# First chunks held by ScalarE, scores by first rows, masks ahead of a running sum, and an opening in needed order

## The chip, the cores and the metric

The kernel runs on one core of a Trainium2 chip. The core has five engines that run side by side and meet only at semaphores: TensorE (PE in the profile; its weight loads are PEld), VectorE (DVE), ScalarE (ACT), GpSimd (POOL) and SyncE (SP), which here only issues transfers. The metric is the time of one execution on the device, in microseconds (us): 380.94 before, the median of 3 runs (380.69 to 381.0).

## The reference

Four batches, eight heads, 768 tokens, 48 channels a head. A gated recurrence gives y, and a feed-forward block with a softmax gate (SoLU) and a layer norm follows:

```python
for t in range(S):
    state = alpha[:, :, t, :, None] * state + np.einsum('bhd,bhe->bhde', k[:, :, t], v[:, :, t])
    y[:, :, t] = np.einsum('bhd,bhde->bhe', q[:, :, t], state)
# x = y, transposed to (3072 tokens, 384)
h = x @ w_in
e = np.exp(h - h_max)
solu = h * e / sum(e)
ln = (solu - mean(solu)) / np.sqrt(var(solu) + 1e-06) * g_ln
out = ln @ w_out
```

The weights `w_in` (384x1024), `w_out` (1024x384) and `g_ln` come as 64-bit floats; everything in the kernel is 32-bit.

## The kernel before, in words

**Groups and chunks.** Time is cut into six groups g of 128 tokens for all four batches b at once (512 columns). The 128 tokens of one batch are a chunk, number n = 4g + b. A group goes through attention, then `up` (h = x times w_in, eight pieces f of 128 hidden units, each with an Exp on ACT, a product on DVE and a Square on ACT: `up_act`), then `down` (four chunks of 128 x 385, each in two halves of four matmuls) and `finish`.

**Attention of a group.** The decay alpha is scanned backwards (`scan_back`, which fills `hT`) and forwards (`scan_on`, in place in `aT`) on DVE. Keys are multiplied by the first scan, queries by the second. The 48 channels of a head are split into 32 "first" rows and 16 "last" rows; tiles have 12 blocks, 8 of first rows (one a head) and 4 with the last rows of two heads. First rows of the queries are `qv[:, 0:8]`; last rows are in `qe`, from which ACT (`apart`) makes two masked copies, for even and for odd heads, in `qv[:, 8:16]`. `scores(g, half)` makes the token by token products of four heads on PE, in four PSUM banks (a0 to a3, one a batch): per head first rows, then last rows added on. `masked(half)` multiplies each bank by a triangle on DVE into `sT`, which frees the bank. `read_state` and `read_values` (L326) then make y from the old state and from `sT`; ACT copies y to `x` (L356), the input of `up`. `next_state` makes the new state; `decay` (GpSimd, L261) multiplies the old one. For `read_state` and `decay`, queries and the ends of the decay are copied by SyncE's transfers into `q64` (lot<-qe by `move_lasts`, lot<-qv by `move_firsts`), a part of the buffer `lot`.

**Getting channels on partitions.** In groups 0 and 1, `turned` transposes k and q on PE (alpha too in group 0), with the last rows gathered by ACT first (`ends_of`); later groups use DVE's transposes (`alpha_T` does it for alpha, with a memset of GpSimd ahead).

**The feed-forward's sums.** `running(g, f)` adds up e and its square over the pieces: one sum on GpSimd, one on DVE (L418). `finish(n)` takes the 385th column of the chunk's result (a sum over hidden units), makes the variance in small DVE instructions (L516 to L521), in group 0 adds the mean's part (L525), takes a power on GpSimd (L529), scales on ACT (L531) and sends the output from SyncE (L532). For group 0, `w_out` isn't centred yet; `centre(f)` does that on GpSimd in group 1.

**Buffers that tie these together.** PSUM has eight banks: two for `h`, two for `o` (results of `down`, also used by other tiles), four `a0` to `a3`. `down(n)` can only begin when the result of chunk n - 2 has been read out of its bank. `o_mean` and `o_sb` have two buffers each, so `finish(n)` reuses those of `finish(n - 2)`.

**What sets the order.** It is written by hand; each engine runs its instructions in program order. Group 0 and the start of group 1 are straight code (L640 to L812). There, the weights come in pieces of 64-bit words into `room` and DVE converts them (`bits`), between all else. From group 1's `up` on, a loop over g and f calls `attend` by a table: `usual`, and `first` for g = 1, say what stands at the head of piece f, behind its `up`, in the middle (after `running`) and at the tail. In the loop's pass g, `up` works on group g and attention on group g + 1, so that the masks and scores named by `first` are those of group 2. `warm` issues matmuls whose results nobody reads.

Of the kernel before, what the change touches and what calls it, by code (L numbers as in the profile page):

```python
# [9 lines left out]
FP = mybir.dt.float32  # L10
# [6 lines left out]
P = 128  # L17
# [15 lines left out]
def fast_path(ctx, tc, q, k, v, alpha, moe_w_in, moe_w_out, moe_g_ln, out):  # L33
# [231 lines left out]
    def quarter(b):  # L265
        return slice(32 * b, 32 * b + 32)
# [4 lines left out]
    def scores(g, half, a=None):  # L271
        a = a or banks("a", [NP, P])
        for i in range(NP):
            h = half * NP + i
            for kb, qb in ((h, h), (H + h // 2, H + h)):
                for b in range(B):
                    nc.tensor.matmul(  # L277
                        a[b][:, i], lhsT=kT[quarter(b), kb], rhs=qv[quarter(b), qb, 0:P], start=kb == h, stop=kb != h,
                        tile_position=(32 * b, 0), skip_group_check=True,
                    )  # L280
        masks[half] = a
# [158 lines left out]
    def warm(n, ps=ps_o, tag="o"):  # L440
        t = ps.tile([P, 512], FP, tag=tag, name="warm")
        for i in range(n):
            nc.tensor.matmul(t[:, 0:P], lhsT=ones, rhs=ones, start=True, stop=True)
# [48 lines left out]
    def down(n, half, part=range(HF)):  # L492
# [4 lines left out]
        for f in (half * HF + i for i in part):  # L497
# [3 lines left out]
            )  # L501

    def finish(n):
        g, b = divmod(n, B)
        d = st[n]
        s, o = sums[:, n], d["o"][:, 0:DM]
        t0 = b * S + g * P
        if g == G - 1:
# [6 lines left out]
            return  # L515
        nc.vector.tensor_copy(out=s[:, 0:1], in_=d["o"][:, DM : DM + 1])  # L516
        t = small.tile([P, 1], FP, name="t")
# [4 lines left out]
        if g == 0:  # L522

            o = work.tile([P, DM], FP, name="o_mean")
            nc.vector.scalar_tensor_tensor(  # L525
                out=o, in0=mean_sb, scalar=s[:, 0:1], in1=d["o"][:, 0:DM], op0=ALU.mult, op1=ALU.add
            )
        r = small.tile([P, 1], FP, name="r")
        nc.gpsimd.tensor_tensor(out=r, in0=s[:, 3:4], in1=mhalf, op=ALU.pow)  # L529
# [136 lines left out]
    def three(name, where):  # L666
        return [pool.tile([P, NP, P], FP, tag=tag, name=f"{name}{i}") for i, (pool, tag) in enumerate(where)]
# [16 lines left out]
    scan_on(0, 0)  # L684
    t = three("tp_q", [(ps_o, "o"), (ps_o, "o"), (ps_a, "a0")])
    turned(qn, ends_of(qn, 3), t)
    for i in (2, 0, 1):
        if i == 1:
            scan_on(0, i)
        part = slice(NP * i, NP * i + NP)  # L690
        nc.vector.tensor_tensor(  # L691
            out=qe[:, :, 0:P] if i == 2 else qv[:, part, 0:P], in0=t[i], in1=aT[:, part, 1:SW], op=ALU.mult
        )
        if i == 2:
            apart()
    warm(2, ps_a, "a1")
    scores(0, 0)
# [79 lines left out]
    move_lasts()  # L777
    finish(0)
    in_range(7)
# [23 lines left out]
    for i in range(3):  # L803
# [5 lines left out]
    down(3, 1, (2, 3))  # L809
    finish(3)  # L810
    scan_on(2, 2)
# [76 lines left out]
    for g in range(1, G + 1):  # L888
# [6 lines left out]

        after = None
        if not rise:
# [520 lines left out]
```

## Time and profile before

| | |
|---|---|
| median of 3 runs | 380.94 us |
| the profiled execution | 380.75 us |
| its span | 378.9 us |
| PE busy | 362.4 us (96%) |
| DVE busy | 246.0 us (65%) |
| ACT busy | 144.7 us (38%) |
| GpSimd busy | 120.5 us (32%) |
| granted TensorE clock, mean | 0.998 |

The span runs from the first to the last instruction that the profiler shows. Times in timelines are from its start. In a timeline a line gives start, length, engine, line of the source, operation, what it writes and reads, shape, count, and in brackets the idle time of the engine before it with what ended it. A wait inside a run of merged instructions doesn't show in brackets. In a table of stretches, each engine has its busy us and its instructions, and the last three numbers are the granted clock, the busy share of the transfer engines and GB/s.

### The profile page before, as it was taken

Reading aid. Unit: us, or ns where it says so; the run is one execution under the profiler, and the core shown is the slowest. Engines: PE = TensorE matmul, PEld = TensorE weight load, DVE = VectorE, ACT = ScalarE, POOL = GpSimd, SP = SyncE. Lnnn points to the kernel's source line nnn. Section 1 sums busy time; section 2 is a strip of 40 time slices with the busy share of each in tenths; the row PEclk is TensorE's granted clock in tenths of the full one; section 3 lists DMA queues with packets and bytes.
Section 4 is the critical chain, followed back from the end, with each engine's and each line's share of the span. In section 5 each row is a group of like instructions: output and inputs, shape, how many; then the busy total and the mean of one; then the engine's idle time right before and its main releaser. Section 6 shows DMA issues by size and latency. Waiting matters only on the chain. (4 is left out here: it accounts for less than half of the span.)

```text
span 378.9 us, 10022 instructions
## 1 busy us (share of the span) xinstructions
PE 362.4 (96%) x4337; PEld 215.1 (57%) x4337; DVE 246.0 (65%) x377; ACT 144.7 (38%) x256; POOL 120.5 (32%) x127
## 2 busy tenths in 40 slices
PE   8789899989999999999999999999999999999994
PEld 8675335656654665555665556565556565555552
DVE  1899878996998879855666855756965314434500
ACT  3628566681255235252341252441341142332101
POOL 7000000010246990775111765112683211333200
PEclk9999999999999999999999999999999999999999
DMA  9982968149149704836033545004041000000011
GB/s 182 189 315 89 210 205 210 43 93 194 59 107 187 172 8 98 155 87 152 22 85 76 114 104 133 24 3 106 0 112 43 24 15 8 22 22 21 27 42 49
DMA packets 72439, 36.06 MB, mean 95 GB/s; under 512 B 48184, under 2 KB 69952, under 8 KB 72384
## 3 DMA queue, kind: packets, MB, share of 16 engines
q1 hardware_dynamic: 71360, 34.39, 38.9%
q10 hardware_dynamic: 1024, 0.92, 0.7%
q8 instruction: 36, 0.59, 0.7%
q14 instruction: 19, 0.16, 0.1%
HBM read 25.30 MB, written 4.72 MB: 79 GB/s over the span
## 5 line engine op out<-in xcount | busy, mean ns | idle before, releaser
L387 PE MATMUL h<-x,w_in 128*128 128x512 f32 x288 | 133.4, 601 | 3.4 <-DVE room L402 2.1
L498 PE MATMUL o<-w_out,room 128*128 128x385 f32 x384 | 133.6, 492 | 0.9 <-DVE o_mean L525 0.9
L498 PEld LDWEIGHTS o<-w_out,room 128*128 128x128 f32 x384 | 71.1, 189 | 55.7 <-issue 13.8
L387 PEld LDWEIGHTS h<-x,w_in 128*128 128x128 f32 x288 | 52.4, 189 | 62.7 <-issue 47.7
L402 DVE TENSOR_TENSOR room<-h,e 128x512 f32<-128x512 f32 x40 | 27.6, 690 | 61.1 <-ACT e L401 61.1
L401 ACT ACTIVATE e<-h 128x512 f32<-128x512 f32 x40 | 23.8, 596 | 96.0 <-PE h L387 95.8
L418 POOL TENSOR_TENSOR p<-p,e 128x512 f32<-128x512 f32 x30 | 41.1, 1369 | 27.6 <-ACT e L401 27.2
L403 ACT ACTIVATE u<-room 128x512 f32<-128x512 f32 x40 | 25.2, 630 | 36.4 <-DVE room L402 36.4
L529 POOL TENSOR_TENSOR r<-sums,mhalf 128x1 f32<-128x1 f32 x20 | 12.2, 608 | 78.4 <-DVE sums L521 78.2
L288 DVE TENSOR_TENSOR sT<-a,mask 128x512 f32<-128x512 f32 x44 | 27.3, 683 | 14.8 <-PE a L277 14.8
L418 DVE TENSOR_TENSOR p<-p,u 128x512 f32<-128x512 f32 x30 | 24.2, 807 | 8.6 <-ACT u L403 8.6
L204 DVE TENSOR_TENSOR_SCAN hT<-aT,unit 128x516 f32<-128x516 f32 x18 | 22.3, 1285 | 7.8 <-ACT aT L674 7.7
L277 PEld LDWEIGHTS a<-qv,kT 32*128 32x128 f32 x704 | 21.9, 186 | 8.7 <-POOL p L418 1.6
L277 PE MATMUL a<-qv,kT 32*128 32x128 f32 x704 | 24.8, 278 | 1.8 <-DVE qv L691 0.8
L212 POOL COPY fend<-hT 128x12 f32<-128x12 f32 x6 | 4.1, 680 | 69.9 <-DVE hT L204 69.9
L204 DVE TENSOR_TENSOR_SCAN aT<-aT,seed 128x516 f32<-128x516 f32 x18 | 25.4, 1442 | 0.2
L326 PE MATMUL y<-sT,vn 128*32 128x128 f32 x768 | 22.9, 274 | 1.0 <-DVE sT L288 0.8
L326 PEld LDWEIGHTS y<-sT,vn 128*32 128x32 f32 x768 | 20.9, 110 | 4.3 <-issue 3.1
L225 POOL TENSOR_TENSOR kT<-kT,hT 128x1024 f32<-128x1024 f32 (+1 forms) x8 | 13.3, 1682 | 22.8 <-DVE kT L179 22.8
L196 ACT ACTIVATE sq<-an,mone 128x1536 uint8<-128x1536 f32 x12 | 18.9, 1574 | 0.2
L531 ACT ACTIVATE o_sb<-o,r 128x384 f32<-128x384 f32 x16 | 9.3, 582 | 24.1 <-POOL r L529 24.1
L356 ACT COPY x<-y 128x384 f32<-128x384 f32 x24 | 11.2, 478 | 14.4 <-PE y L326 14.2
(142 smaller groups left out, 366.0 us busy)
## 6 DMA issues: line engine op xcount, KB each, us to landing
vn<-in_v_dram SPq DMA_DIRECT2D x24, 192.0 KB, 4.3
an<-in_alpha_dram SPq DMA_DIRECT2D x20, 192.0 KB, 4.6
out_dram<-o_sb SPq DMA_DIRECT2D x20, 192.0 KB, 1.9
room<-in_moe_w_in_dram SPq DMA_DIRECT2D x6, 512.0 KB, 7.8
room<-in_moe_w_out_dram SPq DMA_DIRECT2D x8, 384.0 KB, 3.9
kn<-in_k_dram SPq DMA_DIRECT2D x16, 192.0 KB, 4.4
qn<-in_q_dram SPq DMA_DIRECT2D x16, 192.0 KB, 4.9
lot<-qe SPq DMA_DIRECT2D x40, 64.5 KB, 2.1
```

Source lines behind the costliest of these rows:

```text
L196: nc.scalar.activation(out=sq, in_=x, func=AF.Relu, scale=sign, bias=mone, accum_out=over[:, g, i : i + 1])
L204: nc.vector.tensor_tensor_scan(out=o, data0=a, data1=s, initial=1.0, op0=ALU.mult, op1=ALU.add)
L225: nc.gpsimd.tensor_tensor(out=kT[:, part], in0=kT[:, part], in1=hk[:, part], op=ALU.mult)
L277: nc.tensor.matmul(a[b][:, i], lhsT=kT[quarter(b), kb], rhs=qv[quarter(b), qb, 0:P], start=kb == h, stop=kb != h, tile_position=(32 * b, 0 ...
L288: nc.vector.tensor_tensor(out=sT[:, b, half * NP : half * NP + NP], in0=a[b], in1=mask[:, None, :].to_broadcast([P, NP, P]), op=ALU.mult,)
L326: nc.tensor.matmul(y_bank(b)[quarter(r), a], lhsT=lhsT, rhs=rhs, start=(b, r) not in begun, stop=stop, tile_position=(row, 32 * r), skip_g ...
L387: nc.tensor.matmul(h, lhsT=w_in[:, a, f * P : (f + 1) * P], rhs=d["x"][:, a].rearrange("p b t -> p (b t)"), start=(a == 0), stop=(a == KC ...
L401: nc.scalar.activation(out=e, in_=h, func=AF.Exp)
L402: nc.vector.tensor_tensor(out=u, in0=h, in1=e, op=ALU.mult)
L403: nc.scalar.activation(out=u2, in_=u, func=AF.Square)
L418: eng.tensor_tensor(out=p, in0=d[0][i] if f == 1 else p, in1=d[f][i], op=ALU.add)
L498: nc.tensor.matmul(d["o"][:, 0 : DM + 1], lhsT=u_of(g, f)[:, b * P : b * P + P], rhs=w_out[:, f], start=(f == 0), stop=(f == FC - 1), skip ...
```

## The change

Six edits:

1. **Hold.** After the second half of `down(0)` and of `down(1)`, ACT copies the 128 x 385 result out of PSUM into a free part of `lot` (`hold`). `finish(0)` and `finish(1)` then read it there, and stand later: `finish(0)` behind the masks of the first half, `finish(1)` behind those of the second.
2. **Alpha of group 2** (`alpha_T(2)`) is transposed between the two halves' masks, ahead of `finish(1)` and `finish(2)`.
3. **finish(3)** moves from before `scan_on(2, ...)` to after the first `up` of group 1.
4. **Scores.** In each half all four heads' first rows come first, then the last rows of the two even heads, then of the two odd ones. Only the first matmul in a bank carries the starting flag.
5. **Group 2's masks** come right behind their scores, ahead of the centring and of the running sum of pieces 4 and 5, where before they came ahead of the next piece.
6. **Opening.** Queries are turned in the order heads 0 to 3, last rows, heads 4 to 7, into other banks; DVE multiplies heads 0 to 3 before the last rows; four warm matmuls stand ahead of the turning instead of two behind it.

On the engines' queues this moves, besides the instructions named, the power of `finish(0)` and `finish(1)` on GpSimd behind `decay(1)`, their output scalings on ACT behind `in_range(7)`, and the first output's transfer on SyncE behind the four lot<-qv.

```diff
 def scores(g, half, a=None):
-        for i in range(NP):
-            h = half * NP + i
-            for kb, qb in ((h, h), (H + h // 2, H + h)):
+        for last in range(2):
+            for i in (0, 2, 1, 3):
+                h = half * NP + i
+                kb, qb = (H + h // 2, H + h) if last else (h, h)
                 for b in range(B):
                     nc.tensor.matmul(
-                        a[b][:, i], lhsT=kT[quarter(b), kb], rhs=qv[quarter(b), qb, 0:P], start=kb == h, stop=kb != h,
+                        a[b][:, i], lhsT=kT[quarter(b), kb], rhs=qv[quarter(b), qb, 0:P], start=not last and not i, stop=bool(last),
...
+    def hold(n):
+        a = 2 * H * SW + (DM + 1) * (n % 2)
+        st[n]["held"] = lot[:, a : a + DM + 1]
+        nc.scalar.copy(out=st[n]["held"], in_=st[n]["o"][:, 0 : DM + 1])
 def finish(n):
-        s, o = sums[:, n], d["o"][:, 0:DM]
+        s, whole = sums[:, n], d.get("held", d["o"])
+        o = whole[:, 0:DM]
...
-    t = three("tp_q", [(ps_o, "o"), (ps_o, "o"), (ps_a, "a0")])
-    turned(qn, ends_of(qn, 3), t)
-    for i in (2, 0, 1):
+    t = three("tp_q", [(ps_a, "a0"), (ps_o, "o"), (ps_o, "o")])
+    warm(4, ps_a, "a1")
+    turned(qn, ends_of(qn, 3), t, (*range(NP), *range(H, NB), *range(NP, H)))
+    for i in (0, 2, 1):
...
-    warm(2, ps_a, "a1")
     scores(0, 0)
...
     mean(1)
+    hold(0)
     alpha_over(1)
...
     down(1, 1)
+    hold(1)
...
     move_lasts()
-    finish(0)
     in_range(7)
...
     scores(1, 0)
-    finish(1)
     decay(1)
     masked(0)
+    finish(0)
+    alpha_T(2)
     down(2, 1)
     scores(1, 1)
     masked(1)
+    finish(1)
     finish(2)
-    alpha_T(2)
...
     down(3, 1, (2, 3))
-    finish(3)
     scan_on(2, 2)
...
     first = dict(
-        head={3: "keys_back", 5: "masked0", 6: "masked1"},
-        behind={0: "v", 1: "on1", 2: "lasts firsts", 3: "apart", 5: "decay", 7: "alpha back"},
-        tail={4: "scores0", 5: "scores1", 6: "begin read0"},
+        head={3: "keys_back"},
+        behind={
+            0: "v", 1: "on1", 2: "lasts firsts", 3: "apart", 4: "scores0 masked0", 5: "scores1 masked1 decay",
+            7: "alpha back",
+        },
+        tail={6: "begin read0"},
...
-        after = None
+        after = 3 if g == 1 else None
```

More of the change, by code (lines that the diff above doesn't have):

```diff
@@ L515, in finish @@
             return
-        nc.vector.tensor_copy(out=s[:, 0:1], in_=d["o"][:, DM : DM + 1])
+        nc.vector.tensor_copy(out=s[:, 0:1], in_=whole[:, DM : DM + 1])
         t = small.tile([P, 1], FP, name="t")
@@ L522, in finish @@
         if g == 0:
-            o = work.tile([P, DM], FP, name="o_mean")
+            centred = work.tile([P, DM], FP, name="o_mean")
             nc.vector.scalar_tensor_tensor(
-                out=o, in0=mean_sb, scalar=s[:, 0:1], in1=d["o"][:, 0:DM], op0=ALU.mult, op1=ALU.add
+                out=centred, in0=mean_sb, scalar=s[:, 0:1], in1=o, op0=ALU.mult, op1=ALU.add
             )
+            o = centred
         r = small.tile([P, 1], FP, name="r")
```

## The prediction

> **What bounds the kernel now.** I read the page first (busy time by engine), then busy time in stretches of 10 us, then the timelines of PE, DVE, ACT, GpSimd and SyncE wherever PE was not full. Busy time by engine:
>
> ```profile
> PE 362.4 (96%) x4337; PEld 215.1 (57%) x4337; DVE 246.0 (65%) x377; ACT 144.7 (38%) x256; POOL 120.5 (32%) x127
> ```
>
> The stretches (PE's busy us come first, then PEld, DVE, ACT, POOL):
>
> ```profile
> 10.00:20.00 10.00, 7.19 (x221) 6.56 (x225) 9.00 (x12) 6.26 (x9) 0.20 (x1) 1.00 0.96 192
> 20.00:30.00 10.00, 8.92 (x249) 7.91 (x241) 9.45 (x15) 2.76 (x6) 0.12 (x1) 1.00 0.73 275
> 80.00:90.00 10.00, 8.71 (x91) 6.03 (x90) 8.70 (x17) 6.01 (x14) 1.11 (x2) 1.00 0.94 192
> 120.00:130.00 10.00, 9.45 (x110) 5.49 (x112) 7.84 (x11) 4.21 (x8) 9.24 (x8) 1.00 0.71 159
> 150.00:160.00 10.00, 10.00 (x29) 5.11 (x28) 8.40 (x9) 1.83 (x3) 6.63 (x4) 1.00 0.97 179
> ```
>
> From 150 us to the last outputs PE is at 10.00 of 10: nothing can be won there, and whatever starts that stretch earlier ends the kernel earlier by as much. Before it PE idles: in the opening, where DVE is the full engine; at 80 to 100; at 110 to 130. All edits lie in these three. PE's timeline there (start, length, what, and in brackets the idle time before it):
>
> ```profile
> 17.55 0.71 PE L443 MATMUL warm<-ones 128*128 128x128 f32 x4
> 19.10 2.08 PE L277 MATMUL a<-qv,kT 32*128 32x128 f32 x64 [0.84 <-DVE qv L691]
> ...
> 83.06 2.83 PE L498 MATMUL o<-w_out,room 128*128 128x385 f32 x8 [0.89 <-DVE o_mean L525]
> 85.82 0.48 PE L277 MATMUL a<-qv,kT 32*128 32x128 f32 x2
> 86.70 2.06 PE L277 MATMUL a<-qv,kT 32*128 32x128 f32 x62 [0.40 <-DVE sums L516]
> ...
> 97.08 1.01 PE L326 MATMUL y<-lot,state 64*32 64x128 f32 x48 [0.30 <-POOL state L261]
> ...
> 112.95 2.84 PE L387 MATMUL h<-x,w_in 128*128 128x512 f32 x6 [0.31 <-DVE room L402]
> ...
> 123.04 2.01 PE L277 MATMUL a<-qv,kT 32*128 32x128 f32 x56 [0.32 <-ACT qv L245]
> ...
> 127.76 3.44 PE L277 MATMUL a<-qv,kT 32*128 32x128 f32 x64
> ...
> 180.01 2.07 PE L277 MATMUL a<-qv,kT 32*128 32x128 f32 x64
> ```
>
> The last pair matters most: the same 64 instructions take 2.00 us start to start at 180 (180.01 to 182.01) and 3.36 at 127.76 (to 131.12), a wait of 1.36 us that counts as busy. At 122.19 they take 2.79.
>
> SyncE's queue in the second stage, whose copies the state's decay awaits:
>
> ```profile
> 84.10 6.61 SPq L232 DMA_DIRECT2D lot<-qe  x8
> 90.81 0.54 SPq L532 DMA_DIRECT2D out_dram<-o_sb  x1
> 91.48 2.78 SPq L237 DMA_DIRECT2D lot<-qv  x4
> ```
>
> **What the Trainium skill says.** (1) "SBUF — State Buffer", "Who interferes with whom": a VectorE instruction with two SBUF inputs and a GpSimd instruction that reads SBUF block each other. The trace agrees: the running sum L418 takes 0.69 at 120.43 and 1.25 at 122.41, beside a GpSimd sum. (2) "PSUM — Partial Sum Buffer", "The four PSUM rules": a starting matmul clears the written-flags of its whole bank; a later one overwrites where the flag is clear and else accumulates. So one start per bank lets the reordered scores run with as many instructions; no run here shows the flags. (3) "TensorE: Matmul & The Clock Gate", "What's actually happening": the array drops to half clock after an idle window of about 3.4 us. The longest idle here is 1.41 us and the granted clock reads 1.00, so moving the warm matmuls prices at nothing.
>
> **The opening.** DVE is full from 21.20 until 42.8, so the gain is how much earlier its masks begin. Today: `scan_on(0,0)` ends 16.80; DVE idles 0.86 for the third turned tile (PE ends it at 17.6); qe 17.67 to 18.36, qv 18.27 to 18.95; scores 19.10 to 21.1, needing at once the masked copies of ACT (18.39 to 19.73); masks 21.20. After: the turned blocks come as heads 0 to 3, tails, heads 4 to 7. Queries land at 14.80 as before, and the four warm matmuls (about 0.8 us by the 0.71 of two) fit into the 1.41 us wait ahead. With 0.95 us for a third, the first is ready at 15.8, so DVE doesn't idle: qv 16.8 to 17.4, qe to 18.0, ACT's copies 18.05 to 18.7 and 19.4. PE ends turning at 17.6 and starts the 16 first-row products at 17.65; the last rows of even heads follow at 18.75, those of odd heads at 19.45, end 19.95. DVE: scan 17.9 to 19.15, qv 19.2 to 19.9, masks 20.05 instead of 21.20: 1.15 us. Next on DVE is the first weight conversion (25.99, now 24.84), which needs three w_in transfers; the trace's landing records put the last at 24.80. That leaves 0.04 us: I take **1.1 us**, between 0.8 (landing 0.3 later) and 1.15. From there to 80 us compute waits on compute, and loads are issued by compute, so the gain is carried on.
>
> **The second stage, group 1 (times of the old trace, shift left out).** `finish(0)`'s four DVE instructions (81.86 to 82.83, 0.97 us) leave the stretch before the scans; `finish(1)`'s (0.97) leave that before the masks. ACT gets two copies. Their price is that of `mean_sb` (L631, 128x384 from PSUM): 0.48, with the next starting 0.38 after it; upper end 0.59 (a 128x512 copy).
> PE: `down(2,0)` no longer waits 0.89. `scores(1,0)` waits in its second bank for the second qv, which moves from 86.65 to 85.68. So PE is 0.97 earlier through `down(3,0)`, until 95.3. There `read_state(0)` needs the decayed state, and that the last copies of queries: SyncE. `hold(0)` sits ahead of `alpha_over(1)` on ACT, which releases the alpha load (80.23), so that, the qn load and the eight lot<-qe behind them move 0.38 later; they are paced by landings, the last issuing just after qn's at 89.75. The output DMA leaves ahead of lot<-qv, which gives 0.77 back (90.71 to 91.48). Net 0.39 earlier; the 192 KB less ahead of lot<-qv may add 0.1. So of 0.97 PE keeps **0.45**, between 0.15 (copy of 0.59) and 0.8; the rest becomes idle before `read_state(0)`.
> `hold(1)` is done by 81.4, where ACT waited for PE anyway. Behind the masks DVE now does `finish(0)` and the two transposes of `alpha_T(2)` (3.0 us), so masks of the second half run 94.1 to 96.6 instead of 93.57 to 96.05; `read_values` wants them at 100.1, 3.5 us later. If that cover went, each us late would cost PE one. GpSimd's power for `finish(0)` queues behind the decay (ends 96.6): 97.1; its aT memset, for `scan_back`, follows. ACT's outputs 0 to 2 sit ahead of the x copies; output 2 reuses output 0's buffer, so it waits for a landing: issue 97.9 plus 1.9 is 99.8, output 2 ends about 100.5, x copies start at 101.2. Covered by 0.7, and 0.7 more until `up(1,0)`.
>
> **The third stage.** `finish(3)` (3.15 us at 106.82, beside GpSimd's keys) moves behind the first `up`, and DVE comes 2 us earlier to L402: the **0.31** at 112.95 goes. Its output stands before the second Exp on ACT, done 111.6, Exp ready at 112.1: nothing. `scores(2,0)`: first rows need only GpSimd's first queries, and 16 products (1.0 us) cover ACT's masked copies: of 2.79 - 2.00 I take **0.75**. `scores(2,1)`: its banks are freed by the first masks, which today stand behind the running sum (125.50 to 126.62, then masks until 129.1). Ahead of it they run 123.8 to 126.3, while the products ask from 126.05: 0.2 of the 1.36 remains, **1.15** gained. The sum comes after them and is needed only at the end of the group; GpSimd's order there is unchanged.
>
> Later groups get the new scores order where they take 2.00 already: nothing.
>
> **Sum.** 1.1 + 0.45 + 0.31 + 0.75 + 1.15 = 3.76 us. The profiled execution took 380.75 (span 378.9): 376.99. The median 380.94 is 0.19 above it: 377.2.
>
> **Rivals.** (a) GpSimd becomes the bound. It is 9.24 and 9.87 full between 120 and 140, in a chain from the query products to the decay at 131.8. PE now wants that state at 131.2 (133.90 less the 2.66 won since the opening). For: that chain hardly idles. Against: its start hangs on DVE's transposes (117.59), which come about 0.8 earlier, so it ends at 131.0. If it doesn't move, PE waits 0.6: 377.8. (b) The weights bind the opening: landing 1 us later leaves 0.1 of 1.1, 378.2. For: a margin of 0.04. Against: nothing the diff touches issues before them. (c) The SyncE chain eats the second stage: copies of 0.59 and no relief leave 0.15 of 0.45: 377.5. (d) Slower: outputs 0 to 2 sit before the x copies on ACT, and output 2 waits for a landing. Past 101.2 at which a landing begins to bite (1.4 us of slack), each us delays `up(1,0)` by one; to lose all 3.76 and 0.8 more, output 0 would land at 105.8, 8 us after its issue against the median of 1.9. That gives 381.7. (e) The edits don't do what they say, because semaphores rather than data rule: the waits in the built program name exactly these producers, and 380.9 would follow.
>
> **Chances.** Forecast with (c) 0.73 (own range 376.5 to 377.9), (a) 0.10, (b) 0.08, more than forecast (second stage 0.8, all of scores: 376.2) 0.04, (d) 0.03, (e) 0.02. The range to hold 8 in 10: 376.2 to 378.8, where (a) and (b) together make the upper edge. About 0.2% (0.76 us) is what can be told from no change: faster 0.95, same 0.02, slower 0.03.
>
> **What would show it.** Masks from 20.0 with no DVE idle at 17.67; conversion at about 24.8. No wait before `down(2,0)`; idle of 0.5 us before y<-lot,state at about 95. No bracket at the third `up` of group 1; both score blocks near 2.0 to 2.2 us. PE full from 150 on. Wrong if a new wait of over 0.5 us stands before y<-lot,state or h in group 1 to 2, or the conversion waits for w_in.

## The result and the profile after

The changed kernel takes 378.17 us (median of 11 runs, 377.08 to 379.64) where the kernel before took 380.69 beside it (11 runs, 380.30 to 381.38). The ratio is 0.9934, with an interval of 0.9923 to 0.9946: about 2.5 us faster. Forecast were 377.2 us and 3.76 us of gain, so two thirds of the gain came. The profiled execution is one of 378.17 us, its span 376.4. The runs of the changed kernel lie 2.6 us apart, those of before 1.1; that turns out to be part of the story.

The profile after follows in the order of the prediction. Busy time by engine, from the page of the changed kernel:

```profile
PE 362.0 (96%) x4341; PEld 214.9 (57%) x4341; DVE 247.5 (66%) x377; ACT 145.8 (39%) x258; POOL 122.2 (32%) x127
```

Hardly any work was taken off an engine (ACT has the two copies more). Most of the gain is idle time of PE: its span less its busy time was 16.5 us before and is 14.4 now; the rest is waits inside runs of instructions, which count as busy. The stretches of the changed kernel (PE's busy us first, then PEld, DVE, ACT, POOL, clock, share of the transfer engines, GB/s):

```profile
10.00:20.00 10.00, 9.22 (x256) 8.16 (x260) 9.65 (x12) 6.22 (x9) 0.32 (x2) 1.00 0.94 181
80.00:90.00 10.00, 9.40 (x97) 6.27 (x95) 7.79 (x14) 5.11 (x12) 0.00 (x0) 1.00 0.92 196
120.00:130.00 10.00, 10.00 (x142) 6.20 (x141) 8.86 (x13) 4.20 (x7) 9.21 (x8) 1.00 0.68 144
150.00:160.00 10.00, 10.00 (x29) 5.22 (x28) 8.26 (x13) 3.02 (x5) 6.87 (x7) 1.00 0.64 129
```

PE was 7.19, 8.71, 9.45 and 10.00 busy in these before. The clock is still 1.00, so the moved warm matmuls cost none of it. PE's timeline of the changed kernel at the places shown before:

```profile
63.00 2.86 PE L499 MATMUL o<-w_out,room 128*128 128x385 f32 x8
...
81.43 2.76 PE L499 MATMUL o<-w_out,room 128*128 128x385 f32 x8
...
85.19 2.06 PE L278 MATMUL a<-qv,kT 32*128 32x128 f32 x62 [0.60 <-DVE qv L793]
...
95.43 1.82 PE L327 MATMUL y<-lot,state 64*32 64x128 f32 x64 [0.60 <-POOL state L261]
...
98.67 1.42 PE L327 MATMUL y<-lot,state 64*32 64x128 f32 x64
...
105.43 2.74 PE L388 MATMUL h<-x,w_in 128*128 128x512 f32 x6
...
109.60 5.42 PE L388 MATMUL h<-x,w_in 128*128 128x512 f32 x12
...
121.41 2.07 PE L278 MATMUL a<-qv,kT 32*128 32x128 f32 x64
...
126.17 2.21 PE L278 MATMUL a<-qv,kT 32*128 32x128 f32 x64
...
140.35 2.84 PE L388 MATMUL h<-x,w_in 128*128 128x512 f32 x6 [0.60 <-ACT x L357]
...
144.94 0.65 PE L454 MATMUL rows<-p,ones 128*32 128x64 f32 x32 [0.25 <-DVE p L419]
```

The same landmarks in the kernel before, where the prediction's timeline leaves them out:

```profile
63.58 2.86 PE L498 MATMUL o<-w_out,room 128*128 128x385 f32 x8
...
99.51 1.16 PE L326 MATMUL y<-lot,state 64*32 64x128 f32 x64
...
105.63 2.74 PE L387 MATMUL h<-x,w_in 128*128 128x512 f32 x6
...
143.16 2.84 PE L387 MATMUL h<-x,w_in 128*128 128x512 f32 x6 [0.60 <-ACT x L356]
...
147.31 0.64 PE L453 MATMUL rows<-p,ones 128*32 128x64 f32 x32
```

`down(2,0)` waits no more (0.89 before); the idle has moved behind it, 0.60 ahead of y<-lot,state; the wait at the third `up` is gone; both score blocks take 2.0 to 2.1 start to start. New is the wait at rows.

Laid against each other, PE's landmarks give the account, which closes (gain in us; `up(g,f)` is piece f of group g's `up`, "rows" the matmuls that end the running sums, ahead of `down`; "predicted" are the terms of the prediction's sum):

| stretch, by PE's starts | before | after | gain | predicted |
|---|---|---|---|---|
| start to first `down` | 63.58 | 63.00 | 0.58 | 1.1 |
| to `up(1,0)` (second stage) | 42.05 | 42.43 | -0.38 | 0.45 |
| to `up(2,0)` (third stage) | 37.53 | 34.92 | 2.61 | 2.21 |
| to the first rows of group 2 | 4.15 | 4.59 | -0.44 | 0 |
| to the end of the span | 231.59 | 231.46 | 0.13 | 0 |
| sum | | | 2.50 | 3.76 |

The 2.61 is 0.58 at the third `up`, 0.80 at `scores(2,0)` (1.99 instead of 2.79) and 1.22 at `scores(2,1)` (2.14 instead of 3.36). The last row is the claim that whatever starts the full stretch earlier ends the kernel earlier by as much: in all fourteen profiles of this study it lies between 231.30 and 231.59.

The 0.58 at the third `up` is where `finish(3)` had stood; no run moved `finish(3)` alone, so that cause is read from the timelines and not tested.

Three things need a cause: half of the opening's gain is missing, the second stage lost where it should have won, and 0.44 us went ahead of rows.

**The opening.** DVE's timeline of the kernel before, and under it that of the changed kernel:

```profile
21.20 2.48 DVE L288 TENSOR_TENSOR sT<-a,mask 128x512 f32<-128x512 f32 x4 [0.38 <-PE a L277]
...
25.99 0.95 DVE L590 TENSOR_SCALAR lot<-room 128x768 uint32<-128x768 uint32 x1
```

```profile
20.32 2.48 DVE L289 TENSOR_TENSOR sT<-a,mask 128x512 f32<-128x512 f32 x4 [0.24 <-PE a L278]
...
25.48 0.96 DVE L599 TENSOR_SCALAR lot<-room 128x768 uint32<-128x768 uint32 x1 [0.28 <-DMA room<-in_moe_w_in_dram]
```

The masks begin at 20.32, 0.88 earlier than the 21.20 of before (20.05 was forecast). The conversion waits for `w_in`, whose third transfer landed at 25.46 in this execution and at 24.80 in that of before. That is rival (b), with 0.28 us of waiting instead of about 1.

**The second stage.** SyncE's queue of the changed kernel:

```profile
80.03 1.79 SPq L134 DMA_DIRECT2D an<-in_alpha_dram  x4
...
83.90 6.78 SPq L232 DMA_DIRECT2D lot<-qe  x8
90.79 2.47 SPq L237 DMA_DIRECT2D lot<-qv  x4
```

The alpha load is issued 3.62 us after PE starts `tp_q2` (76.41); before it was 3.24 (80.23 less 76.99). That is the 0.38 us by which `hold(0)` was to delay it. The output transfer ahead of lot<-qv is gone as forecast, and PE reaches y<-lot,state 0.26 better than at the first `down`'s start. But from the second read of the state to `up(1,0)` PE then takes 6.76 us instead of 6.12. The trace shows stops of PE's weight loads that wait for nothing it records ("issue" in the brackets). The second read of the state and the end of the read of the values, in the changed kernel (the first two lines are from stretches that end and begin in the stop, 99.54 to 99.69):

```profile
98.67 0.87 PEld L327 LDWEIGHTS y<-lot,state 64*32 64x32 f32 x62 [0.55 <-issue]
99.69 0.14 PEld L327 LDWEIGHTS y<-lot,state 64*32 64x32 f32 x2
...
103.69 0.14 PEld L327 LDWEIGHTS y<-sT,vn 128*32 128x32 f32 x2 [0.24 <-issue]
```

Elsewhere within each of these reads a load starts before the one ahead of it has ended. PE stops after 62 of 64 loads, for 0.15 us, and again after 126 of 128, for 0.24. Between the two stops lie 2 + 126 = 128 pairs of load and matmul, 256 instructions.

**Rows.** DVE's timeline ahead of rows, first of the kernel before, then of the changed kernel, and under it GpSimd's of the changed kernel:

```profile
142.28 3.44 DVE L204 TENSOR_TENSOR_SCAN hT<-aT,unit 128x516 f32<-128x516 f32 x3
```

```profile
139.47 4.73 DVE L204 TENSOR_TENSOR_SCAN hT<-aT,unit 128x516 f32<-128x516 f32 x3
144.13 0.66 DVE L419 TENSOR_TENSOR p<-p,u 128x512 f32<-128x512 f32 x1
```

```profile
136.21 3.63 POOL L643 TENSOR_TENSOR w_out<-w_out,mean_sb 128x384 f32<-128x384 f32 x4
139.79 2.21 POOL L419 TENSOR_TENSOR p<-p,e 128x512 f32<-128x512 f32 x1
```

DVE comes 2.8 us earlier to the three backward scans, as PE does to `up(2,0)`, but GpSimd only 0.3 earlier to its sum (140.08 before). So the scans now run while GpSimd ends its centring and makes its sum (139.79, 2.21 us; 1.28 at 134.92, where no scan runs beside it), and take 4.73 instead of 3.44. DVE's last sum, which rows needs, comes after them.

### The profile page after: what moved, and what is told of

The parts are those of the page before. It is cut to its first block, busy times and chain, and to the rows that moved or that the text cites. A ratio compares the mean times of both kernels' runs of the same rounds, so it can differ in the third digit from the quotient of the medians.

```text
span 376.4 us, 10028 instructions
## 1 busy us (share of the span) xinstructions
PE 362.0 (96%) x4341; PEld 214.9 (57%) x4341; DVE 247.5 (66%) x377; ACT 145.8 (39%) x258; POOL 122.2 (32%) x127
## 5 line engine op out<-in xcount | busy, mean ns | idle before, releaser
L419 POOL TENSOR_TENSOR p<-p,e 128x512 f32<-128x512 f32 x30 | 42.9, 1429 | 27.3 <-ACT e L402 27.0
L204 DVE TENSOR_TENSOR_SCAN hT<-aT,unit 128x516 f32<-128x516 f32 x18 | 23.7, 1359 | 7.7 <-ACT aT L683 7.7
L204 DVE TENSOR_TENSOR_SCAN aT<-aT,seed 128x516 f32<-128x516 f32 x18 | 27.8, 1577 | 0.2
L278 PE MATMUL a<-qv,kT 32*128 32x128 f32 x704 | 23.8, 278 | 0.8 <-DVE qv L793 0.6
L225 POOL TENSOR_TENSOR kT<-kT,hT 128x1024 f32<-128x1024 f32 (+1 forms) x8 | 14.2, 1795 | 20.1 <-DVE kT L179 20.1
```

The lines of the kernel that those rows point to most:

```text
L204: nc.vector.tensor_tensor_scan(out=o, data0=a, data1=s, initial=1.0, op0=ALU.mult, op1=ALU.add)
L225: nc.gpsimd.tensor_tensor(out=kT[:, part], in0=kT[:, part], in1=hk[:, part], op=ALU.mult)
L278: nc.tensor.matmul(a[b][:, i], lhsT=kT[quarter(b), kb], rhs=qv[quarter(b), qb, 0:P], start=not last and not i, stop=bool(last), tile_posit ...
L419: eng.tensor_tensor(out=p, in0=d[0][i] if f == 1 else p, in1=d[f][i], op=ALU.add)
```

## The experiments

Eleven variants ran, and the changed kernel a second time, each compared with runs of the kernel before on the same chip, on three chips in turn: 380.81 us in the first four (11 runs), 381.12 in the second four (26 runs), 380.97 in the last (30 runs). To compare across them I use the ratio to the kernel before; 0.001 is 0.38 us. A ratio's interval is 0.001 to 0.002 to each side, so that a difference of two of them is good to 0.6 to 0.9 us. Each profile is one execution; where it was the fastest or the slowest of its kernel's runs, the text says so.

### The opening undone

```diff
-    t = three("tp_q", [(ps_a, "a0"), (ps_o, "o"), (ps_o, "o")])
-    warm(4, ps_a, "a1")
-    turned(qn, ends_of(qn, 3), t, (*range(NP), *range(H, NB), *range(NP, H)))
-    for i in (0, 2, 1):
+    t = three("tp_q", [(ps_o, "o"), (ps_o, "o"), (ps_a, "a0")])
+    turned(qn, ends_of(qn, 3), t)
+    for i in (2, 0, 1):
...
+    warm(2, ps_a, "a1")
     scores(0, 0)
```

> The changed kernel with the opening as it was before (old order of turning, banks and products, two warm matmuls behind); the rest kept. Theory W (the arrival of the first weights caps the opening): undoing it costs only what the trace shows it won, 0.5 to 0.6 us, so about 378.7; masks start near 21.2, the first conversion near 26.0 with no transfer wait, and the executions spread by about 1 us, since the weights are there in time again. Rival V (the opening is worth the 1.1 us of the prediction and the loss lies elsewhere): 379.3, with the spread of 2.6 us unchanged.

Measured: 378.88 us (378.05 to 380.28), ratio 0.9950 (0.9933 to 0.9966) against 0.9934 with the opening. DVE waits again for the third turned tile, masks begin at 21.22 and the conversion, at 26.01, waits for no transfer. So the opening's part is worth about 0.6 us by these medians, which alone can't exclude 1.1. The profiles can: in the seven of this study with the new opening, the new order of the scores and the old order of the transfers, the conversion begins at 25.05 to 25.72, 25.35 in the mean, and in the two with the old opening and that order at 25.99 and 26.01. That is 0.65 us. The runs still lie 2.2 us apart: the spread is not the opening's alone.

### The weights fetched first

```diff
-    load_v(0)
     fetch(0, 3, 2)
+    load_v(0)
     fetch(2, 1, 2)
```

> The changed kernel with the first three weight transfers issued ahead of the values' four. Theory W: the weights land before 23 us, the first conversion follows the last mask at once (about 25.15 instead of 25.48), no transfer wait before it; 0.3 us faster than the changed kernel at the median, about 377.9, and the executions spread by 1.2 us or less instead of 2.6. Rival V: the conversion is no earlier than about 25.4 or the time stays at 378.2 with the same spread, because the loss and the spread come from elsewhere (for instance PE's instruction supply).

Measured: 377.83 us (377.28 to 378.30), ratio 0.9923 (0.9910 to 0.9936). DVE's timeline of this kernel, where the conversion now follows the masks at once:

```profile
20.38 2.48 DVE L289 TENSOR_TENSOR sT<-a,mask 128x512 f32<-128x512 f32 x4 [0.23 <-PE a L278]
...
25.17 0.96 DVE L599 TENSOR_SCALAR lot<-room 128x768 uint32<-128x768 uint32 x1
```

This profile is of the fastest of the five runs. Masks stand where they stood (20.38, 20.32), the conversion 0.31 earlier: about that much of the opening's miss in the first profile is the weights' landing. The rest is the masks' 0.27. The 0.4 us in the ratio is of that size, though not separable from nothing by these runs. Their spread, 1.0 us, is what the theory expected, of five runs only.

### The same order in the kernel before

> The kernel before with the one edit of fetching the first third of the weights ahead of the values' load. Theory (the weights' landing at 24.80 binds only since the masks come earlier; before, the conversion started at 25.99): no gain, 380.9, ratio 0.999 to 1.001. Rival (the transfers' order helps by itself, the values or the queries landing better too): 0.3 or more faster, 380.6 or less.

The edit is the same, made in the kernel before. Measured: 380.29 us (22 runs, 379.76 to 380.95), ratio 0.9982 (0.9976 to 0.9989), 0.7 us faster. My theory missed: the order of these transfers helps without the change too. In its profile the queries are turned from 14.53 instead of 14.80, the conversion begins at 25.71 without a wait, and the first `down` is 0.48 earlier. So the weights' fetch is not a pure test of rival (b): it seems to move the queries' landing as well. In three of the four profiles with the weights first the second transfer of the queries landed at 14.40 to 14.50 (14.76 in the fourth), in the ten with the values first at 14.68 to 14.95.

### The first copy behind the alpha load's release

```diff
-    hold(0)
     alpha_over(1)
     load(alpha, an, 2)
+    hold(0)
```

> The changed kernel with ScalarE's first copy behind the two passes over alpha that release the next alpha load, instead of ahead of them. Theory Q (SyncE's chain of copies sets read_state, and the copy ahead of it delays it): alpha's load issues 0.37 us earlier, so do lot<-qe and lot<-qv; PE's idle before y<-lot,state falls from 0.6 to about 0.25 and the time by 0.3, to 377.9. Rival: the chain is paced by landings whose times wander by more than that, or PE loses it again before the first up of group 1: 378.2.

Measured: 377.80 us (377.06 to 380.16), ratio 0.9934 (0.9911 to 0.9956). SyncE's queue and then PE's timeline of this kernel:

```profile
79.64 1.79 SPq L134 DMA_DIRECT2D an<-in_alpha_dram  x4
```

```profile
94.87 1.82 PE L327 MATMUL y<-lot,state 64*32 64x128 f32 x64
```

The alpha load is back at 3.24 after `tp_q2`; y<-lot,state follows the first `down` after 31.89 instead of 32.43 and starts without a wait; inside this first read the weight loads still wait 0.36 for the second half of the decayed state. The kernel with all three edits, below, has 31.89 too, the eight other profiles with the copies and the new second stage 32.01 to 32.78. So the chain from the alpha load through lot<-qv to the state did set this point. The ratio shows no gain; the runs scatter too widely (3.1 us) to see 0.4, and this profile is of the fastest of them.

### The sum ahead of the backward scans

```diff
-            7: "alpha back",
...
-        middle={7: "read1 values over"},
+        middle={7: "alpha back read1 values over"},
```

> The changed kernel with group 3's transposes and backward scans moved behind the running sum of piece 7 in group 1. Theory S (the sum is late because the scans, now earlier, run beside GpSimd's centring and are blocked by it): the wait of 0.25 us before rows goes, PE keeps the 0.44 us that it loses between next_state and rows, and the time falls to about 377.75. Rival: the scans move onto the path of group 2 instead and delay a product there by as much: 378.2.

Measured: 378.48 us (377.35 to 379.04), ratio 0.9931 (0.9916 to 0.9946). DVE's timeline and then PE's and GpSimd's of this kernel:

```profile
141.86 3.46 DVE L204 TENSOR_TENSOR_SCAN hT<-aT,unit 128x516 f32<-128x516 f32 x3
```

```profile
131.97 1.02 PE L327 MATMUL y<-lot,state 64*32 64x128 f32 x48 [0.70 <-POOL state L261]
```

```profile
129.83 2.09 POOL L261 TENSOR_TENSOR state<-state,lot 128x384 f32<-128x384 f32 x2 [1.33 <-DMA lot<-qv]
```

The scans take 3.46 us again, and rows follows `up(2,0)` after 4.17 us instead of 4.59: with the scans behind the sum that loss is gone, and its cause is shown. The time didn't fall with it, since in the profiled execution the state of group 2 waited 1.33 us for lot<-qv and PE 0.70 for the state. In the changed kernel that wait was 0.71 and just covered; before, there was none. It is the third place where the change has brought compute up to a transfer.

### The masks undone

```diff
-        head={3: "keys_back"},
-        behind={
-            0: "v", 1: "on1", 2: "lasts firsts", 3: "apart", 4: "scores0 masked0", 5: "scores1 masked1 decay",
-            7: "alpha back",
-        },
-        tail={6: "begin read0"},
+        head={3: "keys_back", 5: "masked0", 6: "masked1"},
+        behind={0: "v", 1: "on1", 2: "lasts firsts", 3: "apart", 5: "decay", 7: "alpha back"},
+        tail={4: "scores0", 5: "scores1", 6: "begin read0"},
```

> The changed kernel with the masks of the third stage where they were before the change (the first half's masks ahead of piece 5, the second half's ahead of piece 6, the scores behind pieces 4 and 5, the running sum between). Theory (banks are freed late by the masks): the 64 products of scores(2,1) take about 3.3 us start to start instead of 2.14 and nothing later gives it back, so 378.2 + 1.2 = 379.4. Rival (the transfers of group 2 give part of it back): lot<-qv lands near 129.5 in any order, so a later PE finds the decayed state ready and no wait follows at the rows; only about 0.5 of the 1.2 shows, 378.7.

Measured: 379.42 us (378.61 to 380.74), ratio 0.9963 (0.9950 to 0.9975), so 1.1 us slower than with the change. PE's timeline of this kernel:

```profile
126.02 3.75 PE L278 MATMUL a<-qv,kT 32*128 32x128 f32 x64 [0.27 <-DVE sT L289]
129.69 2.84 PE L388 MATMUL h<-x,w_in 128*128 128x512 f32 x6
```

The block takes 3.67 start to start and starts 0.35 late: 1.9 lost in this profile. Rows gets 0.44 back, because DVE comes later to its scans again (4.15 from `up(2,0)` to rows). The total is the theory's, but its "nothing later gives it back" was wrong, and its 3.3 for the block too low. The rival, that transfers would give half back, did not hold.

### The order of the scores undone

```diff
-        for last in range(2):
-            for i in (0, 2, 1, 3):
-                h = half * NP + i
-                kb, qb = (H + h // 2, H + h) if last else (h, h)
+        for i in range(NP):
+            h = half * NP + i
+            for kb, qb in ((h, h), (H + h // 2, H + h)):
```

> The changed kernel with the products of the scores in their old order (head after head, both key blocks together) in all groups. Theory: in the opening the products need the masked copies and the second queries at once, so the first masks come at about 20.9 instead of 20.32, but the first conversion still waits for w_in near 25.4, so nothing of that shows at the first up product; scores(2,0) again waits for its masked copies and takes about 2.7 us instead of 1.99. Sum +0.7: 378.9. Rival (order of the products without worth, since its queries arrive in the needed order anyway): scores(2,0) stays at 2.0 to 2.2, and the time at 378.2.

Measured: 379.27 us (378.30 to 381.27), ratio 0.9955 (0.9941 to 0.9969), 0.8 us slower. PE's timeline of this kernel:

```profile
18.03 0.50 PE L277 MATMUL a<-qv,kT 32*128 32x128 f32 x8 [0.36 <-DVE qv L700]
19.38 2.02 PE L277 MATMUL a<-qv,kT 32*128 32x128 f32 x56 [0.85 <-ACT qv L245]
...
122.58 0.50 PE L277 MATMUL a<-qv,kT 32*128 32x128 f32 x8
123.24 2.01 PE L277 MATMUL a<-qv,kT 32*128 32x128 f32 x56 [0.15 <-ACT qv L245]
```

The total is near what was expected, its place not: the opening doesn't swallow its part. (By this profile 2.0 us are lost; it is of an execution of 380.18, 0.9 above the median.) Waiting 0.85 for the masked copies, its masks begin at 21.42 and end at 26.3, and the conversion follows at 26.21 without a wait, later than in the kernel before (25.99). So in this profile the opening's new order of the queries is worth nothing without the new order of the scores. `scores(2,0)` takes 2.60 start to start, 0.6 more than with the new order, for the masked copies.

### The two copies undone

```diff
-    hold(0)
     alpha_over(1)
...
-    hold(1)
...
     move_lasts()
+    finish(0)
...
     scores(1, 0)
+    finish(1)
     decay(1)
     masked(0)
-    finish(0)
     alpha_T(2)
...
     masked(1)
-    finish(1)
     finish(2)
```

> The changed kernel without the two copies by ScalarE: the first two outputs of group 1 are finished in their old places, all else as changed. Theory of the prediction (SyncE's chain sets y<-lot,state): down(2,0) waits about 0.9 again and starts about 0.97 later, but y<-lot,state comes only 0.3 to 0.5 later, because lot<-qe is issued 0.38 earlier. Since the stretch from read_state to up(1,0) is 0.2 to 0.6 shorter where PE comes with pauses, up(1,0) moves by 0 to 0.3, and the time is 378.2 to 378.5. Rival (the copies are worth their whole 0.97): y<-lot,state and up(1,0) come 0.97 later, 379.1. Second rival (the copies cost more than they bring): up(1,0) comes 0.3 earlier, 377.9.

Measured: 378.67 us (378.46 to 379.98), ratio 0.9934 (0.9920 to 0.9949), the same as with the copies. PE's timeline of this kernel:

```profile
82.61 2.83 PE L499 MATMUL o<-w_out,room 128*128 128x385 f32 x8 [0.86 <-DVE o_mean L533]
...
96.33 0.55 PE L327 MATMUL y<-lot,state 64*32 64x128 f32 x16 [0.45 <-POOL state L261]
```

`down(2,0)` waits 0.86 again, y<-lot,state comes 0.74 later than in the changed kernel (from the first `down`), not the 0.3 to 0.5 of the theory; lot<-qe took 7.14 us here instead of 6.78. The stop in the second read is here too (0.42, behind the 61st load). From the first `down` to `up(1,0)` it is 43.28 us, 0.85 more than with the copies. Then 0.70 more is lost at the state of group 2, whose transfers waited 1.45. But this profiled execution took 379.98 us, the slowest of its five runs and 1.3 more than their median, so its landmarks are not those of the usual run. The medians say that the copies bring nothing that these runs can see; a gain of half a us could hide in them.

### Three edits together

Weights first, `hold(0)` late and the sum ahead of the scans, in the changed kernel.

> The changed kernel with three edits: the weights' fetch ahead of the values' load, hold(0) behind the alpha load's release, and the scan_back of group 2 behind GpSimd's centring. If the three act on separate places their gains of 0.34, 0.37 and 0.44 at PE's landmarks add up: 378.2 - 1.15 = 377.0, with up(1,0) near 104.2. Rival (the landing of lot<-qv in group 2 is now the bound): PE waits 0.5 or more before y<-lot,state of group 2 at about 130, and the sum shrinks to the gain that is left there, about 0.5: 377.7.

Measured: 377.60 us (376.50 to 378.13), ratio 0.9907 (0.9891 to 0.9923): 1.0 us better than the changed kernel against the same reference, near the 1.15 of the sum, and the lowest ratio of this study. PE's timeline of this kernel:

```profile
94.79 1.82 PE L327 MATMUL y<-lot,state 64*32 64x128 f32 x64
...
104.17 2.74 PE L388 MATMUL h<-x,w_in 128*128 128x512 f32 x6
...
143.29 0.65 PE L454 MATMUL rows<-p,ones 128*32 128x64 f32 x32
```

No wait ahead of y<-lot,state nor at rows, no stop in the read (6.14 us), and `up(1,0)` at the 104.2 that was expected. The state of group 2 waited 0.75 for its transfer, covered. This profile is of the fastest of the six runs (376.50, 1.1 below the median).

### The three edits without the copies

> The kernel with all three edits (weights first, hold(0) behind the alpha load's release, scan_back behind the centring) without ScalarE's two copies, outputs 0 and 1 of group 1 finished in their old places. Theory of the chain: the copies no longer delay the alpha load in the kernel with all three, so that they are worth their 0.97 there less what the 192 KB output ahead of lot<-qv costs: this kernel is 0.6 to 0.9 slower than the one with all three, 378.3 to 378.5. Rival (what the copies win is given back before the third stage in any case, as it seemed where hold(0) was late by nothing): within 0.2 of it, 377.6 to 377.8.

Measured: 377.74 us (377.10 to 379.77), ratio 0.9909 (0.9894 to 0.9924), 0.1 from the kernel with the copies. The rival held. GpSimd's timeline of this kernel:

```profile
131.10 2.13 POOL L261 TENSOR_TENSOR state<-state,lot 128x384 f32<-128x384 f32 x2 [1.89 <-DMA lot<-qv]
```

Its profiled execution (379.77) is again the slowest of its runs, 2.0 above the median, with that wait of 1.89 and 0.95 of PE's behind it. So by the profiles the copies seem worth 0.85 at `up(1,0)` in the one pair and 2.17 in the other, and by the medians 0.0 and 0.1, each good to about 0.8. The medians decide: no gain of the copies is shown, and none of the forecast's 0.45 is excluded. Where the 0.97 us saved ahead of `down(2,0)` goes in a usual run without them, no profile here shows.

### The instruction stream moved by six pairs

```diff
-    warm(14)
+    warm(17)
```

> The changed kernel with 17 instead of 14 warm matmuls ahead of the first transposes, where TensorE waits for alpha to land (six more pairs of weight load and matmul, about 1.0 us of a wait of 1.2). Theory (the small stops of TensorE in the second read of the state and in the read of the values sit at fixed places of its instruction stream): they move six pairs forward, from 62 to 56 of the 64 and from 126 to 120 of the 128 pairs, and the time stays at 378.2. Rival (they belong to the operands or to the copies of outputs that leave at that time): they stay at 62 of 64 and 126 of 128, or come at no fixed place.

Measured: 378.93 us (377.46 to 380.61), ratio 0.9955 (0.9934 to 0.9975); the difference to the changed kernel, 0.8 us, is what two such intervals leave open. PE's weight loads in the second read of the state, from stretches that end and begin in the stop:

```profile
99.00 0.82 PEld L327 LDWEIGHTS y<-lot,state 64*32 64x32 f32 x56 [0.55 <-issue]
99.97 0.15 PEld L327 LDWEIGHTS y<-lot,state 64*32 64x32 f32 x8
```

Six pairs added more than 90 us earlier, and the stop has moved from behind load 62 to behind load 56. In the opening's read of the values it moved from behind the 27th load to behind the 21st. In the read of group 1's values no stop shows this time. With the opening undone, whose stream is two warm matmuls (four pairs) shorter, it lies three pairs later, behind the first load of the values. The missing pair is found when TensorE's own waiting instructions are counted too, which the timelines leave out: ahead of the stop the traces have 1369 pairs and 15 of them in the changed kernel, 1369 and 15 with the six pairs, 1368 and 17 with the opening undone or the copies undone. That is 2753 instructions each time; the stop in the read of the values lies 256 instructions behind that, and one in the first read of the state, in two profiles, 256 ahead. So the stops sit at places of the instruction stream, not at operands. They are not there each time: a stop stands in the second read of the state in nine of the 14 profiles, in the read of the values behind it alone in two more, and in neither read in the two with the old second stage nor in that with all three edits. The page of the changed kernel has a queue for instructions:

```profile
q8 instruction: 36, 0.59, 0.7%
```

That is 36 pieces of 16 KB, and PE's 4341 loads and 4341 matmuls are about 34 times 256. The Trainium skill, "Runtime: NRT & Kernel Launch", section "Instruction fetch mechanics", states that an engine's instructions are refilled in blocks of 16 KiB, 256 instructions, and that crossing a boundary is mostly hidden. The 256 between two stops agree. Hidden it is in the second stage's reads of the kernel with all three edits, and perhaps of the kernel before, where the count puts the crossing between the two reads and 0.20 us stand in every profile; in those of the changed kernel two crossings cost about 0.6 us together.

Why a block is late in one execution and not in another is settled in part. In the opening's read of the values a stop of 0.07 to 0.91 us stands in all ten profiles with the values' load ahead of the weights, and in none of the four with the weights first: there the order of the transfers decides. In the second stage it stays open. Outputs on their way are hardly the reason: with all three edits two of them are under way beside the second read (96.72 to 98.62 and 97.68 to 99.61) and there is no stop, and without the copies one alone (98.42 to 100.83), with a stop of 0.42.

### The changed kernel again

> The changed kernel itself again, for a second profile beside the three others on one chip. Theory (the landings of the first queries, of w_in and of lot<-qv wander between executions, and the change has brought compute up to them): first up at 29.8 to 30.4, y<-lot,state of group 1 at 94.8 to 95.9, state of group 2 waiting 0 to 1.4 for lot<-qv; median 378.2 with a spread of over 2 us. The stops of TensorE at 62 of 64 and 126 of 128 pairs come again at the same places. Rival (the profile of the changed kernel shows fixed costs): all landmarks within 0.1 of the first profile's.

Measured: 377.75 us (377.18 to 380.40), ratio 0.9930 (0.9905 to 0.9955). In the second profile (an execution of 377.18) the masks begin at 20.27, the conversion at 25.05 without a wait, the first `up` at 29.72 instead of 30.16, y<-lot,state at 94.83 with 0.64 idle, and the state of group 2 waits 0.32. It is the fastest of these six runs. The stop is at 62 of 64 again, that at 126 of 128 isn't there. So the opening's wait and the size of the loss at rows (4.31 here, 4.59 in the first profile, against 4.15) wander. In the seven profiles named above, with the new opening and the old order of the transfers, the conversion waited for `w_in` in five, 0.07 to 0.28 us, and in two not.

The loss in the second stage doesn't wander: from the first `down` to `up(1,0)` eight profiles with the changed kernel's second stage have 42.22 to 42.49, the two with that of before 42.05 and 42.07, those with `hold(0)` late 41.58 and 41.26, those without the copies 43.28 and 43.44. In the eight, the two parts of it trade: the sooner y<-lot,state follows the first `down` (32.01 to 32.78), the longer it takes from the second read to `up(1,0)` (7.03 to 6.35). Time won ahead of the reads is spent in the stop.

## Why the prediction was right, and where its sum was off

The time lies in the wide range, 376.2 to 378.8, but not in the likeliest case's own, 376.5 to 377.9; it stands where rival (b) had put it, at 378.2, and only 0.3 us of it is that rival. The sum missed by 1.26 us: the opening fell short by 0.52 and the second stage by 0.83, rows took 0.44 that was not in it, and the third stage gave 0.40 more than forecast (the last 0.13 is in the full stretch). That surplus was luck, and so was it that the kernel before ran at 380.69 beside it and not at the 380.94 of the forecast. Two of the prediction's own signs of being wrong came: the conversion waits for `w_in`, and 0.60 us stand before y<-lot,state, though "over 0.5" was an ill-chosen sign where it expected 0.5.

**What bounds the kernel.** Right: PE's idle ahead of 150 us is what the change could win, and the stretch behind it keeps its length to 0.3 us in fourteen profiles.

**The opening: right mechanism, wrong size.** 0.58 by the first profiles, 0.6 by undoing it and 0.65 at the conversion in the mean, where 1.1 was forecast with 0.8 as the lower end. The step that failed is "masks 20.05 instead of 21.20" (20.32, since the last products end later than my 19.95) together with "the trace's landing records put the last at 24.80. That leaves 0.04 us". A margin of 0.04 was no margin against a landing that came at 24.80 to 25.76 in the ten profiles with that order of transfers. Some waiting was to be expected in most executions, and the likeliest value had none.

**The second stage: a gain that was not carried on.** Right were the freed wait of `down(2,0)`, the 0.38 us by which `hold(0)` delays the alpha load, SyncE's chain as what sets y<-lot,state, and the idle of 0.5 there (0.60). At y<-lot,state the gain was 0.26, within the bounds of 0.15 to 0.8. The step that failed is "of 0.97 PE keeps **0.45**": the reads behind y<-lot,state take 0.64 more, about 0.6 of it in the two stops. I had priced PE's reads as fixed, without a reason. Instead of 0.45, the stage measured -0.38, and taking the copies out changes the time by 0.0 and 0.1 us, within what the runs can tell. Of the prediction's own terms, the 0.97 us that leave the stretch before the scans are there, and no gain in time is shown for them.

**The third stage: right.** 0.80 and 1.22 against 0.75 and 1.15; undoing the parts costs 1.1 (masks) and 0.8 (order of the scores, part of it in the opening). The 0.31 at the third `up` measured 0.58. A bracket counts from the end of the matmuls ahead, and where nothing holds PE the next ones start about 0.2 before that end (pieces of 2.84 us, two of them in 5.25 from 109.60 on), so the wait there was 0.5 all along. That DVE's earlier arrival comes from moving `finish(3)`, and what the move of `alpha_T(2)` is worth, no run tested alone.

**Rows: a term left out.** "The sum comes after them and is needed only at the end of the group; GpSimd's order there is unchanged" looked at the sum, not at what DVE's earlier arrival does to the scans behind it. What the prediction cites from the Trainium skill, "SBUF — State Buffer", "Who interferes with whom", it applied to the sum only. (Beside the sum's 1.25 at 122.41 stood GpSimd's products of the queries, 120.68 to 123.11, more than a GpSimd sum; the reading holds.) The scans read two SBUF operands as well, and went from 3.44 to 4.73 us for three, 0.44 us at rows in that profile and 0.05 to 0.44 in the others. Moving the sum ahead of them removed it. With the copies undone it was GpSimd that was held: the scans took 3.40 and its sum beside them 5.32. So engines meet not only at semaphores, as the part on the chip has it.

**The rivals.** (a) didn't happen as told: PE did not wait for the state of group 2. But GpSimd did stay behind the others, and the 0.44 at rows is where it showed. And what stands there is the transfer lot<-qv, with 0.1 to 1.9 us of waiting on GpSimd in eleven of the profiles, and in four variants it reached PE (0.15, 0.70, 0.70 and, put down to the transfer of the next queries, 0.95). (b) happened in the first profile, 0.3 of its 1. (c) named the right stage, and its 0.15 was still too much, but not for its reason: the gain at y<-lot,state was 0.26. (d) is visible, output 2 waited 1.65 us for a landing and the x copies began at 101.18, and PE did not wait for them at `up(1,0)`, with the cover of 0.7 that was forecast. (e) is excluded.

## What to carry to other kernels

When an edit takes a compute wait away, ask of each place further on which transfer or which neighbour's work compute now meets, and give a margin below the wander of a landing (0.6 us between two executions of one kernel here) a real chance rather than a zero. An engine that arrives earlier somewhere also arrives earlier beside another engine: check what it will share there, as the scans did with GpSimd. And once a kernel's runs spread over 2 to 3 us, one profile tells mechanisms but not sizes; undo each part, compare medians, and run often enough that their interval is smaller than the term in question.

## What I had not expected of the hardware

- PE's weight loads stop at places fixed in its instruction stream, a multiple of 256 instructions apart, for 0.07 to 0.91 us each, in some executions; six pairs of instructions added at the start move the place by six.
- In the opening the order of two loads of data decides whether such a stop comes: in ten of ten profiles with the values first, in none of four with the weights first.
- Three scans of 128x516 on DVE take 3.41 to 3.48 us in the six profiles in which GpSimd rests beside them and 4.38 to 4.77 in seven in which it works, its sum going from 1.28 to 2.21 us in the changed kernel; in one, the scans take 3.40 and the sum 5.32.
- The same transfer lands 0.6 us apart in two executions of one kernel: the third `w_in` transfer at 25.46 and 24.86. The wait for lot<-qv in group 2 is 0.71 and 0.32 in the same two.
- Fetching 1.5 MB of weights ahead of the values' load made the kernel before 0.7 us faster (interval 0.4 to 0.9), though the conversion it feeds had 1.2 us to spare.
